# Linear attention and a mixer block on one core: spans of 384 and 288, tensor-engine tiles of 32 and 64 rows or columns, a new instruction order

## The chip, the cores and the metric

The kernel runs on one core of a Trainium2 chip. The metric is device time in microseconds (us). The engines are named as the profile names them: PE is the tensor engine's matrix multiply and PEld its weight load, DVE the vector engine, ACT the scalar engine, POOL the GpSimd engine, SP the engine that issues all DMAs here.

## The reference

Batch 4, 4 heads, sequence 1088, head dimension 32; the mixer works on 128 channels (4 heads of 32), with 256 token units and 1536 channel units.

```python
def phi(x):                                  # 8 x 8 = 64 features of one head
    a = np.einsum('rd,bhsd->bhsr', S1, x)
    b = np.einsum('rd,bhsd->bhsr', S2, x)
    return np.einsum('bhsi,bhsj->bhsij', a, b).reshape(*x.shape[:-1], r * r)
q_p, k_p = (phi(q), phi(k))
kv = np.einsum('bhsf,bhsd->bhfd', k_p, v)
z = np.sum(k_p, axis=2)
num = np.einsum('bhsf,bhfd->bhsd', q_p, kv)
den = np.einsum('bhsf,bhf->bhs', q_p, z)[..., None] + 1e-06
x = num / den                                # then (B, S, H * D)
h = np.maximum(x.T @ w_tok1, 0.0) @ w_tok2   # token mixing, per batch
u = x + h.T
out = u + np.maximum(u @ w_ch1, 0.0) @ w_ch2 # channel mixing
```

The four mixer weights arrive as 64-bit floats and are made into 32-bit floats on the chip.

## The kernel before

Every piece of work is an operation with a short name, a cost per engine and a list of what it depends on (`Plan.add`, L153). The order of all operations is written out by hand in the list `ORDER` (L62): `Plan.run` (L166) goes through it, emits each operation on its engine, and adds fills (`fill`, L269: matmuls of the identity into a spare bank) where its costs expect PE idle for more than 400 ns. Each engine then runs its own queue in that order and waits on semaphores. Names with a suffix (`:pool`, `:dve`) say which engine takes an operation that either could do.

The stages, with the names that the text uses:

- **Weights.** 17 pieces of 64-bit words, `w00` to `w04` (first token weight, tiles of 128 rows), `w10` to `w15` (second), `w20` to `w22` and `w30` to `w32` (the two channel weights). Each is loaded (`d00` and so on, L276; the tile is called `doubles`) and converted (`convert`, L283) in six steps: ACT takes the magnitude of the high word (`abs`, L293) and scales the low word (`low`, L297); DVE clamps (`clamp`, L300), shifts into PSUM (`shift`, L304) and puts the sign on (`merge`, L307); POOL adds the two (`add`, L311 and L313). Later each weight is divided into a high and a low half for fast matmuls (`hi` on ACT, L394; `lo` on DVE or POOL, L397).
- **Keys**, `K0` to `K3`, one per batch (`keys`, L411): projections (`K.p`, L424), products on DVE (`K.v`, L443), and sums over the sequence (`K.s`, L460), 36 matmuls each of 64 output rows by 66 columns: for head h the values of both heads of its pair are multiplied, and `blocks` (L470) keeps the half that belongs to the head.
- **Queries.** Batch 0 on PE (`Q0.p`, L539, 12 matmuls with all 128 rows of the transposed queries; the stationary operand `s_spread` is zero for the rows of other heads), with products `Q0.m` on DVE (L560) or POOL (L557). Batches 1 to 3 project 64 rows (`Q.p`, L505, 4 matmuls of 64 x 272), write them to memory (`Q.w`, L599) and read them back repeated (`Q.r`, L612 and L615), then multiply (`Q.m`, L625).
- **Attention and token mixing**, `A0` to `A3` (`mixing`): `A.x` (L645, 36 matmuls), the division `A.d` on DVE, `A.t` (L695 in batch 0, L701 after), `A.w` (L817, L821), residuals `A0.u` (L726), and the division of u into halves, `uh` on ACT (L792) and `ul` on DVE or POOL (L795).
- **Channel mixing**, `U0` to `U11` (`channel_mix`, L856): the 4352 columns of all batches are cut into 12 spans (`_spans`, L40): 384, 384, 320 for batch 0, then eight of 384 and one of 192. For each span and each of 12 blocks of 128 hidden units: three matmuls (`f`, L871), a ReLU into a high part on ACT (`h`, L875), the low part on DVE (`l`, L878), three matmuls (`s`, L884). A span ends with an addition (`ol`, L909) and its store (`out`, L920).

A matmul of 32-bit floats shows as two MATMUL records in the profile, one of the divided halves as one.

Of the kernel before, what the change touches and what calls it, by code (L numbers as in the profile page):

```python
# [67 lines left out]
A0.x0 w03.add Q0.a21 Q0.b21 w10.low w11.abs w20.abs Q0.m21 A0.x1 w04.shift w10.shift A0.d0 A0.d1 w04.merge w11.clamp w04.add w10.merge w11.shift
w20.clamp w11.merge Q1.p Q1.c0 w11.low w30.low w10.add w11.add w13.low w12.abs Q1.c1 w30.abs w20.low w12.low w13.abs A0.x2 A0.d2 A0.t0 A0.t1 A0.t2
A0.relu A0.hT A0.hTh A0.u0 A0.w0 k1 d21 d31 Q1.w0 v1 Q1.w1 d14 d15 d22 d32 q2 w20.shift w12.clamp w30.clamp w20.merge w13.clamp w12.shift w30.shift  # L70
w12.merge w13.shift w30.merge w20.add w20.hi A0.uh00 K1.p w12.add w20.lo:dve w30.add A0.ul00 w13.merge U0.f U0.f A0.u1 U0.f w13.add A0.w1 w00.hi K1.c0
# [919 lines left out]
```

## Time and profile before

| what | value |
|---|---|
| time, median of 3 runs | 224.02 us (223.56 to 224.95) |
| time of the profiled execution | 224.45 us |
| its span, first to last instruction | 222.6 us |
| granted PE clock over the span | 1.000 |
| PE busy | 216.7 us, 97% |
| DVE busy | 151.1 us, 68% |
| ACT, POOL busy | 115.0 us, 60.7 us |

The profiled execution is one run of the program; its time is 1.85 us longer than the span that the instructions cover. Busy time of an engine is the time during which at least one of its instructions is in flight, so a PE that is busy 97% need not be at its peak.

### The profile page before, as it was taken

To read this page: it belongs to the slowest core of one execution; us is meant where nothing else is said; L and a number is where in the kernel's file an instruction comes from. 1 tells how busy PE (TensorE), PEld (TensorE's weight loads), DVE (VectorE), ACT (ScalarE), POOL (GpSimd) and SP (SyncE) were. 2 spreads that over 40 slices of the span, in tenths; PEclk is the share of its full clock that TensorE was granted. 3 is DMA by queue.
4 is the path that set the end of the run, shared out by engine and by line. 5 is a ranking of instruction groups with operands and counts; after the bars stand their busy time and mean duration, and the time that the engine had idled before them with its cause. 6 is when DMAs were issued, how large, how long until landed. Compare 5 with 4: busy or idle time off the path is not lost.

```text
span 222.6 us, 4807 instructions
## 1 busy us (share of the span) xinstructions
PE 216.7 (97%) x1854; PEld 205.5 (92%) x1854; DVE 151.1 (68%) x310; ACT 115.0 (52%) x269; POOL 60.7 (27%) x62
## 2 busy tenths in 40 slices
PE   7999999999999999999999999999999999999994
PEld 7767868789899999999999999999999999999994
DVE  2599999999779854786644667384556654665652
ACT  3488859865826343444533437253554455445441
POOL 2256585578961615102120505000000000000000
PEclk9999999999999999999999999999999999999999
DMA  6999899697059884249550100035000000020001
GB/s 193 417 406 406 248 361 349 214 259 213 9 116 170 256 167 79 65 111 172 197 168 0 38 0 3 0 141 141 3 0 3 35 3 0 0 71 3 35 0 53
DMA packets 10726, 28.41 MB, mean 128 GB/s; under 512 B 1360, under 2 KB 4688, under 8 KB 10704
## 3 DMA queue, kind: packets, MB, share of 16 engines
q1 hardware_dynamic: 10704, 28.11, 41.5%
q8 instruction: 14, 0.23, 0.4%
q14 instruction: 8, 0.07, 0.1%
HBM read 23.27 MB, written 4.83 MB: 126 GB/s over the span
## 4 chain that ended last, share of the span: by engine, by line
PE 79%; DMA 6%; DVE 6%; ACT 3%; issue 2%; SPq 1%; POOL 1%; POOLq 0%; ACTq 0%
PE ps_o L884 29%; PE ps_h L871 28%; DMA br<-rows 5%; PE ps_a L821 4%; PE ps_a L701 3%; PE ps_o L272 3%; PE ps_a L645 3%; PE ps_a L460 2%; DMA doubles<-wt 2%; DVE hl L878 2%; PE ps_a L539 1%; PE ps_h L539 1%; DVE k_p L443 1%; ACT tail L297 1%; PE ps_o L460 1%
## 5 line engine op out<-in xcount | busy, mean ns | idle before, releaser
L875 ACT ACTIVATE hh<-ps_h 128x384 fp32r<-128x384 f32 (+2 forms) x144 | 68.2, 475 | 84.4 <-PE ps_h L871 63.3
L878 DVE SCALAR_TENSOR_TENSOR hl<-ps_h,hh 128x384 fp32r<-128x384 f32 (+2 forms) x144 | 75.3, 532 | 50.3 <-ACT hh L875 46.0
L871 PE MATMUL ps_h<-uh,halves 128*128 128x384 f32 (+2 forms) x288 | 86.0, 333 | 0.6 <-DVE hl L878 0.5
L884 PE MATMUL ps_o<-hh,halves 128*128 128x384 f32 (+2 forms) x288 | 72.0, 332 | 0.0
L871 PEld LDWEIGHTS ps_h<-uh,halves 128*128 128x128 f32 x288 | 53.1, 188 | 1.8 <-DVE hl L878 1.0
L884 PEld LDWEIGHTS ps_o<-hh,halves 128*128 128x128 f32 x288 | 50.6, 188 | 0.6
L871 PE MATMUL ps_h<-ul,halves 128*128 128x384 f32 (+2 forms) x144 | 47.4, 329 | 0.0
L884 PE MATMUL ps_o<-hl,halves 128*128 128x384 f32 (+2 forms) x144 | 47.4, 329 | 0.0
L871 PEld LDWEIGHTS ps_h<-ul,halves 128*128 128x128 f32 x144 | 27.1, 188 | 0.0
L884 PEld LDWEIGHTS ps_o<-hl,halves 128*128 128x128 f32 x144 | 27.1, 188 | 0.0
L625 POOL TENSOR_TENSOR qp<-qp,br 128x544 f32<-128x544 f32 x9 | 13.2, 1484 | 15.9 <-DMA br<-rows 8.7
L311 POOL TENSOR_TENSOR whole<-c,tail 128x512 int32<-128x512 int32 (+3 forms) x11 | 11.7, 1063 | 9.6 <-DVE c L307 8.1
L669 POOL TENSOR_TENSOR xl<-x,xh 128x384 fp32r<-128x384 f32 x6 | 6.1, 1017 | 28.6 <-ACT xh L665 28.6
L293 ACT ACTIVATE c<-doubles 128x512 f32<-128x512 f32 (+3 forms) x17 | 10.3, 624 | 2.5 <-DMA doubles<-wt 2.5
L443 DVE TENSOR_TENSOR k_p<-ps_a,a_sb 128x1024 f32<-128x1024 f32 (+1 forms) x12 | 11.0, 947 | 0.0
L307 DVE SCALAR_TENSOR_TENSOR c<-doubles,ps_h 128x512 int32<-128x512 int32 (+3 forms) x17 | 10.4, 610 | 0.2
L297 ACT ACTIVATE tail<-doubles 128x512 int32<-128x512 uint32 (+3 forms) x17 | 10.4, 630 | 0.1
L304 DVE TENSOR_SCALAR ps_h<-c 128x512 int32<-128x512 int32 (+3 forms) x17 | 10.3, 615 | 0.1
L645 PEld LDWEIGHTS ps_a<-kvz,qp 128*64 128x64 f32 x288 | 9.0, 137 | 1.3 <-issue 0.5
L701 PE MATMUL ps_a<-halves,xh 128*128 128x256 f32 x54 | 10.0, 279 | 0.0
L300 DVE TENSOR_SCALAR c<-c 128x512 f32<-128x512 f32 (+3 forms) x17 | 8.6, 522 | 2.0 <-ACT c L293 1.9
L313 POOL TENSOR_TENSOR c<-c,tail 128x512 int32<-128x512 int32 x6 | 8.1, 1358 | 6.6 <-DVE c L307 3.2
(82 smaller groups left out, 242.2 us busy)
## 6 DMA issues: line engine op xcount, KB each, us to landing
qp<-rows SPq DMA_DIRECT2D x6, 544.0 KB, 8.6
br<-rows SPq DMA_DIRECT2D x12, 272.0 KB
doubles<-wc SPq DMA_DIRECT2D x6, 512.0 KB, 10.8
v_sb<-v SPq DMA_DIRECT2D x4, 594.0 KB, 4.6
k_sb<-kT SPq DMA_DIRECT2D x4, 576.0 KB
q_sb<-qT SPq DMA_DIRECT2D x4, 544.0 KB, 10.4
doubles<-wt SPq DMA_DIRECT2D x4, 512.0 KB, 7.0
xm<-xb SPq DMA_DIRECT2D x3, 576.0 KB, 9.2
```

Of the source, the lines that this page charges most:

```text
L293: nc.scalar.activation(f32(t["c"]), f32(high), AF.Abs)
L297: nc.scalar.activation(t["tail"], low.bitcast(U32), AF.Copy, scale=2.0 ** -29)
L307: nc.vector.scalar_tensor_tensor(t["c"], high, -(1 << 30), t["ps"], op0=ALU.bitwise_and, op1=ALU.bitwise_or)
L311: engines[e].tensor_tensor(dst(), t["c"], t["tail"], op=ALU.add)
L443: nc.vector.tensor_tensor(t["k_p"][:pn, t0 * H:t1 * H], a.unsqueeze(3).broadcast_to([pn, n, R, R]), t["sb", t0][:pn, :n].unsqueeze(2).broa ...
L625: engines[e].tensor_tensor(qp[:, p, cs], qp[:, p, cs], t["br"][:, p, cs], op=ALU.mult)
L645: nc.tensor.matmul(x_ps[c:c + 64, o:o + 2 * (D + 1)], lhsT=qp[:, p, s0 + c:s0 + c + 64], rhs=kvz_all[b % 2][:, p, :], start=True, stop=True,)
L701: nc.tensor.matmul(t["h_ps"][:, :DTOK], lhsT=t[l][:m, i, :], rhs=part(0, piece, r, j * DTOK, DTOK)[:m], start=(i == 0 and k == 0), stop=(i ...
L871: nc.tensor.matmul(h_ps[:, :cn], lhsT=part(2, at[2][e][0], l, at[2][e][1] * P, P), rhs=r[:, :cn], start=(m == 0), stop=(m == 2))
L875: nc.scalar.activation(t["hh"][:, :cn], t["h"][:, :cn], AF.Relu)
L878: nc.vector.scalar_tensor_tensor(t["hl"][:, :cn], t["h"][:, :cn], 0.0, f32(t["hh"][:, :cn]), op0=ALU.max, op1=ALU.subtract)
L884: nc.tensor.matmul(outs[i][:, :cn], lhsT=part(3, at[3][e][0], l, at[3][e][1] * P, P), rhs=r[:, :cn], start=(e == 0 and m == 0), stop=(e == ...
```

## The change

- The last spans: seven of 384 and two of 288 in place of eight of 384 and one of 192.
- `K.s`: each head is multiplied with its own 33 value columns, not with the 66 of its pair. For batches 1 to 3 the 64 features of a head are cut into two matmuls of 32 output rows (72 matmuls of 32 x 33 in place of 36 of 64 x 66). Batch 0 keeps 36, of 64 x 33.
- `Q.p` of batches 1 to 3: eight matmuls of 64 input rows by 32 output rows in place of four of 128 by 64. `Q0.p`: the two head pairs are projected in one operation, each from its own 64 rows, in place of one pair at a time from all 128.
- The conversion: `shift` is gone; `sign` (the sign bit of the high word into PSUM) depends on the load alone; `clamp` has one operation in place of two; `merge` shifts and joins.
- Fills may be 512 columns wide; 36 matmuls of 32 x 8 stand at the program's start.
- Loads have no fixed order among themselves any more, and `ORDER` is another list. The low halves of w20, w12, w01, w10 and w15 move from DVE to POOL with it.

```diff
-    for n in (384,) * 8 + (192,):
+    for n in (384,) * 7 + (288, 288):
...
-s d00 q0 k0 d01 v0 d02 d03 d04 d10 d11 d20 d30 q1 d12 d13 s.abs s.low s.clamp s.shift s.merge s.add Q0.s0:dve Q0.s1:pool w00.abs w00.low w00.clamp
+s q0 d00 d04 d01 k0 s.low s.abs s.clamp s.sign s.merge s.add Q0.s0:dve Q0.s1:dve Q0.p00 Q0.a00 Q0.p01 w00.sign w00.abs Q0.m00 Q0.b01 w00.clamp w04.abs
...
+PAD = 36
...
-            for _ in range(n):
-                nc.tensor.matmul(spare_ps[:, :P], lhsT=ident, rhs=ident, start=True, stop=True)
+            for w in [4] * (n // 4) + [1] * (n % 4):
+                nc.tensor.matmul(spare_ps[:, :w * P], lhsT=ident, rhs=ident.unsqueeze(1).broadcast_to([P, w, P]), start=True, stop=True)
...
-        op = plan.add(name, {"sp": 475.0}, emit, (), takes, uses, boost, order=after)
+        op = plan.add(name, {"sp": 475.0}, emit, (), takes, uses, boost)
...
+        def sign(e):
+            t["ps"] = bank("ps_h")[:, :n].bitcast(I32)
...
+                nc.vector.tensor_scalar(t["ps"], high, -(1 << 31), None, op0=ALU.bitwise_and)
         def clamp(_):
-            nc.vector.tensor_scalar(f32(t["c"]), f32(t["c"]), LEAST, MOST, op0=ALU.max, op1=ALU.min)
-
-        def shift(_):
-            t["ps"] = bank("ps_h").bitcast(I32)[:, :n]
-            nc.vector.tensor_scalar(t["ps"], t["c"], 3, 0x3FFFFFFF, op0=ALU.logical_shift_left, op1=ALU.bitwise_and)
+            nc.vector.tensor_scalar_min(f32(t["c"]), f32(t["c"]), MOST)
         def merge(_):
-            nc.vector.scalar_tensor_tensor(t["c"], high, -(1 << 30), t["ps"], op0=ALU.bitwise_and, op1=ALU.bitwise_or)
+            nc.vector.scalar_tensor_tensor(t["c"], t["c"], 3, t["ps"], op0=ALU.logical_shift_left, op1=ALU.bitwise_or)
...
-                        nc.tensor.matmul(
-                            t["kv"][j * F:(j + 1) * F, p * 2 * (D + 1):(p + 1) * 2 * (D + 1)],
-                            lhsT=t["k_p"][:n, i * H + h].rearrange("p i j -> p (i j)"),
-                            rhs=t["v"][:n, i, 2 * p:2 * p + 2, :].rearrange("p h d -> p (h d)"),
+                        for c in range(parts):
+                            o, m = j * F + c * F // parts, F // parts
+                            nc.tensor.matmul(
+                                t["kv"][o:o + m, p * (D + 1):(p + 1) * (D + 1)],
+                                lhsT=t["k_p"][:n, i * H + h, c * R // parts:(c + 1) * R // parts].rearrange("p i j -> p (i j)"),
+                                rhs=t["v"][:n, i, h, :], start=(i == 0), stop=(i == NT - 1),
...
-        for j in range(2):
-            c = 2 * j + r
-            nc.tensor.matmul(ps[j * 64:(j + 1) * 64, :QC], lhsT=box["s_rows"], rhs=q[:, c * QC:(c + 1) * QC], start=True, stop=True)
+        for c in range(4):
+            for p in range(2):
+                rows = slice(p * 64, (p + 1) * 64)
+                nc.tensor.matmul(ps[p][c * 32:(c + 1) * 32, :QC], lhsT=box["s_rows"][rows], rhs=q[rows, c * QC:(c + 1) * QC], start=True, stop=True)
...
-                        nc.tensor.matmul(x[:, :cn], lhsT=t["s"][:, kind, 2 * p:2 * p + 2].rearrange("p h i j -> p (h i j)"), rhs=box["q_sb", 0][:, cs], start=True, stop=True)
+                        nc.tensor.matmul(
+                            t[kind, g, p][:, :cn], lhsT=t["s"][rows, kind, 2 * p:2 * p + 2].rearrange("p h i j -> p (h i j)"),
+                            rhs=box["q_sb", 0][rows, cs], start=True, stop=True,
...
+    for i in range(PAD):
+        c = i % 4 * 32
+        nc.tensor.matmul(spare_ps[c:c + 32, :8], lhsT=ident[:, c:c + 32], rhs=ident[:, :8], start=True, stop=True)
```

The new list moves instructions. Three places follow. In them `doubles_90` is piece w30, `doubles_91` w12, `doubles_92` w13 and `doubles_93` w21; L305 is `sign`, L308 `clamp`, L311 `merge`, L447 the key products and L817 `ul` in the kernel after, L304, L300, L307, L443 and L795 their counterparts before.

First, DVE just ahead of and behind the first `ul` of span U0. Before:

```order
L307 SCALAR_TENSOR_TENSOR c<-doubles_91,ps_h 128x384
L304 TENSOR_SCALAR ps_h<-c 128x384
L307 SCALAR_TENSOR_TENSOR c<-doubles_90,ps_h 128x512
L397 TENSOR_TENSOR halves_465<-c,halves_465 128x512
L795 TENSOR_TENSOR ul<-ps_a,uh 128x384
L307 SCALAR_TENSOR_TENSOR c<-doubles_92,ps_h 128x384
L443 TENSOR_TENSOR k_p<-ps_a,a_sb 128x1024
```

And now:

```order
L305 TENSOR_SCALAR ps_h<-doubles_92 128x384
L305 TENSOR_SCALAR ps_h<-doubles_93 128x512
L305 TENSOR_SCALAR ps_h<-doubles_90 128x512
L311 SCALAR_TENSOR_TENSOR c<-c,ps_h 128x384
L447 TENSOR_TENSOR k_p<-ps_a,a_sb 128x1024
L308 TENSOR_SCALAR c<-c 128x512 x2
L311 SCALAR_TENSOR_TENSOR c<-c,ps_h 128x512
L817 TENSOR_TENSOR ul<-ps_a,uh 128x384
L311 SCALAR_TENSOR_TENSOR c<-c,ps_h 128x512
```

The merge of w13, the first product of K1, and the sign and the clamp of w21 moved ahead of `ul`; the low half of w20 (`halves_465`) left DVE.

Second, PE around the same place, from the transposes of the hidden units of batch 0 (L735 before) to the first channel matmuls (L871 before); `whole` is a converted piece of the second token weight. Before:

```order
L735 MATMUL ps_a<-ident,h 128x128 x2
L726 MATMUL ps_a<-ident,x 128x128 x3
L817 MATMUL ps_a<-whole_376,hTl 128x384
L817 MATMUL ps_a<-whole_378,hTl 128x384
L424 MATMUL ps_a<-s_c,k_sb 64x64 x18
L871 MATMUL ps_h<-uh,halves_465 128x384
L871 MATMUL ps_h<-ul,halves_465 128x384
```

And now (L757, L428, L748, L839 and L893 are the counterparts of L735, L424, L726, L817 and L871):

```order
L757 MATMUL ps_a<-ident,h 128x128 x2
L428 MATMUL ps_a<-s_c,k_sb 64x64 x18
L748 MATMUL ps_a<-ident,x 128x128 x3
L839 MATMUL ps_a<-whole_506,hTl 128x384
L839 MATMUL ps_a<-whole_432,hTl 128x384
L748 MATMUL ps_a<-ident,x 128x128 x3
L839 MATMUL ps_a<-whole_519,hTl 128x384
L839 MATMUL ps_a<-whole_528,hTl 128x384
L893 MATMUL ps_h<-uh,halves_552 128x384
L893 MATMUL ps_h<-ul,halves_552 128x384
```

The second transposes and the second token product of batch 0, which stood behind the first channel matmuls, now stand ahead of them.

Third, PE at the projection of Q2 and the sums of K1. Before:

```order
L871 MATMUL ps_h<-uh,halves_465 128x384
L505 MATMUL ps_a<-q_sb,s_rows 64x272 x4
L460 MATMUL ps_a<-v_sb,k_p 64x66 x36
L424 MATMUL ps_a<-s_c,k_sb 64x64 x18
L871 MATMUL ps_h<-uh,halves_465 128x384
```

And now:

```order
L893 MATMUL ps_h<-uh,halves_552 128x384
L512 MATMUL ps_a<-q_sb,s_rows 32x272 x8
L467 MATMUL ps_a<-v_sb,k_p 32x33 x72
L893 MATMUL ps_h<-uh,halves_552 128x384
```

The projection and the sums have twice the matmuls, of smaller tiles, and the projection of K2 (L424) has left this place for a later one of its own.

## Rows read from the trace of the kernel before

**Rows 1.** The page: busy time, share and instructions of each engine.

```profile
PE 216.7 (97%) x1854; PEld 205.5 (92%) x1854; DVE 151.1 (68%) x310; ACT 115.0 (52%) x269; POOL 60.7 (27%) x62
```

**Rows 2.** Busy time of each engine in stretches of 10 us.

```profile
core 0: us, PE busy (x) PEld busy (x) DVE busy (x) ACT busy (x) POOL busy (x), PEclk, DMA share, GB/s
...
30.00:40.00 10.00, 10.00 (x101) 8.17 (x101) 9.97 (x19) 8.73 (x22) 6.20 (x6) 1.00 0.98 345
40.00:50.00 10.00, 9.36 (x131) 8.45 (x127) 9.72 (x18) 7.29 (x20) 7.26 (x6) 1.00 0.82 245
50.00:60.00 10.00, 10.00 (x115) 9.26 (x113) 8.86 (x14) 7.59 (x19) 8.98 (x8) 1.00 0.44 124
```

**Rows 3.** The chain of waits from 31 to 48 us, by line.

```profile
by line: DMA doubles<-wt 23.1%; DVE hl L878 20.1%; issue 17.8%; DVE k_p L443 15.3%; DVE c L300 11.9%; DVE c L307 10.9%; DVE ps_h L304 9.0%; DVE ul L795 6.4%; PE ps_h L871 4.7%; PE ps_o L884 1.0%
```

**Rows 4.** Timeline from 0 to 11 us: start, length, instruction, idle time before it.

```profile
1.36 6.70 PE L272 MATMUL ps_o<-ident 128*128 128x128 f32 x32 [1.36 <-POOL ident masks.py:199]
...
5.54 0.67 ACT L293 ACTIVATE c<-doubles 128x512 f32<-128x512 f32 x1 [2.54 <-DMA doubles<-wt]
...
7.90 0.81 PE L539 MATMUL ps_a<-q_sb,s_spread 128*128 128x384 f32 x2
...
9.46 0.56 DVE L560 TENSOR_TENSOR qp<-xT,ps_h 128x384 f32<-128x384 f32 x1 [1.34 <-PE ps_h L539]
...
10.54 0.49 DVE L560 TENSOR_TENSOR qp<-xT,ps_h 128x320 f32<-128x320 f32 x1 [0.52 <-PE ps_h L539]
```

**Rows 5.** Timeline from 30 to 38 us, DVE.

```profile
30.89 0.73 DVE L397 TENSOR_TENSOR halves<-c,halves 128x512 fp32r<-128x512 f32 x1
31.54 0.55 DVE L795 TENSOR_TENSOR ul<-ps_a,uh 128x384 fp32r<-128x384 f32 x1
32.01 0.54 DVE L307 SCALAR_TENSOR_TENSOR c<-doubles,ps_h 128x384 int32<-128x384 int32 x1
...
34.87 0.42 DVE L300 TENSOR_SCALAR c<-c 128x512 f32<-128x512 f32 x1
...
35.67 0.68 DVE L304 TENSOR_SCALAR ps_h<-c 128x512 int32<-128x512 int32 x1
...
37.32 1.22 DVE L443 TENSOR_TENSOR k_p<-ps_a,a_sb 128x1024 f32<-128x1024 f32 x1
```

**Rows 6.** Timeline from 31.5 to 35 us, PE.

```profile
31.97 0.44 PE L871 MATMUL ps_h<-uh,halves 128*128 128x384 f32 x1
...
33.12 0.49 PE L726 MATMUL ps_a<-ident,x 128*128 128x128 f32 x3
...
33.98 1.45 PE L817 MATMUL ps_a<-whole,hTl 128*128 128x384 f32 x4
```

**Rows 7.** The chain of waits in order of time, whole program: start, length, what.

```profile
8.06 0.65 PE ps_a L539 x2
...
15.70 2.27 PE ps_o L460 x72
...
56.74 2.25 PE ps_a L460 x72
58.99 0.72 PE ps_o L884 x3
...
80.38 0.88 PE ps_h L871 x6
81.26 1.07 PE ps_a L505 x8
...
204.21 1.56 PE ps_o L884 x9
...
218.19 1.35 PE ps_o L884 x12
```

**Rows 8.** Timeline from 11.60 to 11.70 us, PE.

```profile
11.65 0.28 PE L424 MATMUL ps_a<-s_c,k_sb 128*64 128x64 f32 x2
```

**Rows 9.** Line L424 by itself: count, shortest, median and longest in ns, first and last start.

```profile
L424 PE MATMUL ps_a<-s_c,k_sb x144: 220/222/270, 11.7 to 66.3; 128*64 128x64 f32 x144
```

**Rows 10.** Timeline from 54 to 56 us, POOL.

```profile
54.42 1.30 POOL L397 TENSOR_TENSOR halves<-whole,halves 128x512 fp32r<-128x512 f32 x1
```

More of the change, by code (lines that the diff above doesn't have):

```diff
@@ L68 @@
[L68 to L71, printed above, removed]
@@ new lines @@
+w04.clamp w00.merge Q0.p20 Q0.p21 Q0.a01 Q0.a20 Q0.p10 Q0.m01 Q0.m20 s.rows w01.abs Q0.a21 Q0.a10 K0.p d02 w04.low Q0.b21 w04.sign w01.clamp w01.sign
+w04.merge w01.merge w02.sign v0 d03 d11 d20 d10 d12 d13 k1 q1 d21 d30 Q0.p11 Q0.m21 w00.low w00.add w04.add K0.c0 w02.low K0.c4 K0.c8 w01.low w01.add
+K0.v0 Q0.m10 K0.v4 K0.v8 w02.abs w03.abs w02.clamp w03.clamp w02.merge w03.low Q0.a11 w11.abs Q0.b11 w11.clamp w03.sign w11.sign Q0.m11 w03.merge
+w02.add w11.merge K0.s00 K0.s04 K0.s08 K0.s10 K0.s14 K0.s18 K0.kvz A0.x0 w10.abs A0.d0 A0.x1 A0.d1 A0.x2 A0.t0 A0.t1 w03.add A0.d2 w10.sign w11.low
@@ new lines @@
+Q1.p w11.add w12.abs w13.abs w10.low w20.abs w20.low Q1.c0 Q1.c1 A0.t2 A0.relu A0.hT w10.clamp w13.clamp w12.clamp w20.sign w20.clamp w12.sign
+w10.merge d31 d14 Q1.w0 q2 v1 Q1.w1 w20.merge w12.merge K1.p d15 d32 d22 Q1.r0None Q1.r00 Q1.r01 Q1.r1None Q1.r10 Q1.r11 w10.add w20.add w13.low
+w12.low w30.abs A0.hTh K1.c0 w12.add w13.sign w21.sign w30.sign w13.merge w13.add K1.v0 A0.u0 A0.w0 A0.u1 A0.w1 w21.low K1.c4 w30.low w21.abs w20.hi
+A0.uh00 w30.clamp w21.clamp w20.lo:pool w30.merge A0.ul00 w21.merge w31.abs w31.low w13.hi K1.c8 K1.v4 K1.v8 U0.f U0.f U0.f w30.add A0.uh11 U0.h U0.h
@@ new lines @@
+w30.hi w21.add Q2.p A0.ul11 w31.clamp U0.l U0.l w31.sign w31.merge w30.lo:pool K1.s U1.f U0.h w14.low w21.hi w21.lo:pool w14.abs w15.abs U1.h U0.l
+w31.add U1.l w14.sign w22.low w22.abs Q2.c0 w14.clamp w15.clamp w14.merge U0.s U1.f U0.s U0.s U1.f U1.s U0.f U1.h w31.hi U1.h w15.low U0.h Q2.c1
+w00.hi U1.l w22.clamp w15.sign U1.l U0.l w15.merge w31.lo:pool w14.add w22.sign w22.merge U1.s A0.u2 U1.s U0.s U0.f U0.f w15.add A0.w2 U0.h w01.hi
+U0.h w32.abs w32.low U0.l w22.add w32.sign U0.l w32.clamp w32.merge w22.hi Q1.m00:pool w22.lo:pool w32.add Q1.m10:pool Q1.m01:pool U0.s U1.f U1.f U0.s
@@ L316, in convert @@
         r = plan.add(name + ".low", act_sb(n), rest, [loaded], [tail_hold])
+        g = plan.add(name + ".sign", dve(n), sign, [loaded], [ps_hold])
         m = plan.add(name + ".clamp", dve2(n), clamp, [a], (), [c_hold], port=True)
[L318 to L319 removed]
+        m = plan.add(name + ".merge", dve(n), merge, [m, g], (), [c_hold, ps_hold])
         ways = {"dve": 69 + 2.084 * n} if keep else {"pool": 141 + 2.15 * n}
@@ L583, in project @@
                 t["ps", r] = bank("ps_a")
-                project_queries(box["q_sb", b], r, t["ps", r])
-        p = plan.add(f"{n}.p", {"pe": 2 * 2 * QC / 1.2}, project, [q_loaded[b], s_rows_done], ps, [q_hold[b]], boost, 1, order=[after])
+            project_queries(box["q_sb", b], [t["ps", r] for r in range(2)])
+        p = plan.add(f"{n}.p", {"pe": 2 * (QC / 1.2 + 40)}, project, [q_loaded[b], s_rows_done], ps, [q_hold[b]], boost, 2, order=[after])
         for r in range(2):
```

141 lines of the change are left out of this document (73 added, 68 removed).

## The prediction

> **What bounds the kernel now.** I read the page first: PE is busy 97% of the span [rows 1], so at first sight the time is the sum of PE's work. The table of stretches splits this. From 30 to 50 us DVE is busy 9.97 and 9.72 of 10 us, and PE shows 9.36 in the second of these [rows 2]. The chain of waits for 31 to 48 us runs almost wholly over DVE lines and the loads, with 4.7% and 1.0% on PE [rows 3]: PE's queue is full there, but with instructions that DVE releases. From 50 us on PE is busy 10.00 [rows 2], and the end of the chain is PE alone [rows 7]. So I cut the time at the first channel matmul of span U0, at 31.97 us [rows 6]. What comes before is set by DVE, which has to convert weights; what comes after is mainly PE's own work; its last matmul ends at 218.19 + 1.35 = 219.54 us [rows 7]. That leaves 222.6 - 219.54 = 3.06 us for the last addition and store. So before = 31.97 + 187.57 + 3.06.
>
> **The middle: PE's work behind the first channel matmul.**
>
> *Spans.* Three matmuls per block, two layers, 12 blocks make 72 matmuls for a span. One of 384 columns takes 1.56 / 9 = 0.1733 us, one of 320 takes 0.88 / 6 = 0.1467, one of 192 takes 1.35 / 12 = 0.1125 [rows 7]. A 384 and a 192 cost 72 x 0.2858 = 20.6 us. For 288 the line through 384 and 320 gives 0.1334, the line through 320 and 192 0.1382, so two spans of 288 cost 19.2 to 19.9 us. The gain is 0.7 to 1.4; I take 1.3, since 288 is nearer to 320.
>
> *Sums of K1 to K3.* They cost 2.25 us each, 72 records, 36 rounds with two tiles abreast, 0.0625 us a round [rows 7]. The query projection, also two abreast, takes 1.07 / 4 = 0.2675 us a round with 272 columns [rows 7]. Time goes with columns: (0.2675 - 0.0625) / (272 - 66) = 1.0 ns a column and nothing fixed. With 33 columns a round takes about 0.031 us; 144 records at four abreast are 36 rounds, 1.1 us. No row shows four tiles abreast. The other end is that a record costs 2.25 / 72 = 0.031 us however small it is: 144 x 0.031 = 4.5 us. Between the ends, two records of different tiles start close together: two took 0.28 us in all [rows 8], where one lasts up to 0.270 [rows 9], so some 10 ns apart; four in 40 ns would give 1.4 us. I take 1.2, near to the column rule: 3 x 1.05 = 3.15 us gained; the ends are a gain of 3.4 and a loss of 6.8.
>
> [...]
>
> *Projections Q2 and Q3.* Eight tiles abreast make two rounds of 0.2675, 0.53 us in place of 1.07. Tiles that share columns and differ in rows occur nowhere in this trace, so the ends are 0.5 gained each and, if row tiles took turns, nothing. I take 2 x 0.53 = 1.06 gained.
>
> *Work that moves ahead of the cut.* One transposed residual, at most 0.49, less what overlaps, about 0.3, and one token product: four records of 384 columns at 0.65 a pair, 1.3 us [rows 6, 7]. 1.6 us leave the middle.
>
> *Changes of tile shape.* Behind the sums three second-layer matmuls take 0.72 where 3 x 0.1733 = 0.52 are due [rows 7], so a change costs about 0.2 us. By the order the middle had 14 such changes and now has 18: K2's projection stands alone, and projection and sums, adjacent twice, differ in shape. That costs 0.8.
>
> *Waits on DVE.* PE sits visibly idle for 0.64 us from 40 to 50 us [rows 2]. The order now converts w13 and most of w21 ahead of the cut, so I let this go.
>
> Middle: 187.57 - 1.3 - 3.15 - 1.06 - 1.6 + 0.8 - 0.64 = 180.6 us.
>
> **The front: when the first channel matmul can run.** PE's savings here (Q0.p halved, 12 matmuls of about 0.65 us, 0.54 for the short ones; K0.s halved from 2.27 us [rows 7]) need not show, because DVE decides. DVE runs two long conversions of the front behind each other and its first `ul` ends at 32.09 us [rows 5]. To its list ahead of that `ul` the order adds the sign of w21 (0.68, as a `shift` of that size), its clamp (0.42), the merge of w13 (0.54) and K1's first product (1.22); it takes off the low half of w20 (0.73) [rows 5]: +2.1 us. `sign` costs what `shift` cost, same size and destination; the clamp is as long with one operation as with two, as far as I can bound it (0 to 0.42 less). Off the list go waits: DVE sat idle 1.34 and 0.52 us for the first query products [rows 4]. Those came late because 32 records of fills held PE until 7.90 us [rows 4]. At 6.70 / 16 = 0.42 us a fill, the seven fills' worth that remain ahead of Q0, with 36 small matmuls of some 0.5 to 1.3 us, let it start near 5.5 us if the queries have landed, and they are now loaded first. But the first weight, which had landed by 5.54 [rows 4], comes behind them. I take half of the 1.86 us, 0.9. The cut moves to 31.97 + 2.1 - 0.9 = 33.2 us; ends 31.3 (all idle gone and overlap of instructions counted) and 35.
>
> Free loads and the shorter chain from load to merge I cost at nothing: DVE's full queue covers them. If that cover were gone, each would pull the front forward, and the second rival prices that. `clamp` and `merge` now wait for ACT and for `sign`; what is queued behind them on DVE is more conversions, and ahead of the cut only PE waits for those, with fills.
>
> **The tail.** The last addition has 288 columns, not 192, and the store half as many bytes again: +0.1, 3.16 us.
>
> **The sum.** 33.2 + 180.6 + 3.16 = 217.0 us of span. The profiled execution took 224.45 for a span of 222.6, and the median of the runs lies 0.43 under the profiled one; so 217.0 + 1.85 - 0.43 = 218.4 us. The likeliest case has its own range of 216 to 221.
>
> **The rivals.**
>
> *PE sets the front too.* From 7.90 to 31.97 PE spent 24.1 us. Without 3.6 of Q0.p, 1.1 of K0.s and 0.5 of Q1.p, with the 1.6 that moved in and nine more changes of shape (1.8), it needs 22.3 us from 5.5 on: the cut at 28 to 30, 4 us earlier, and 214.5 us in all. For it: PE is also busy in the front. Against it: DVE's 9.97 of 10 [rows 2], and DVE's list grew. Chance 0.22.
>
> *Small tiles are paced by their number.* At 0.031 us a record the sums take 4.5 us, 3.3 more than I count, three times: 218.4 + 9.9 = 228.3, slower. It decides from a sum of 1.2 + 5.6 / 3 = 3.1 us on, where the whole gain is gone. For it: 31 ns a record is what the trace shows on average. Against it: the proportion to columns, and two records 10 ns apart [rows 8, 9]. [...] Chance 0.10.
>
> *POOL becomes late.* Five low halves (512, 384, 512, 384 and 320 columns) move to POOL, where 512 take 1.30 us [rows 10]: 2112 / 512 x 1.30 = 5.4 us. POOL was busy 8.98 of 10 us from 50 to 60 [rows 2], and `A1.t` and `A1.w` wait for these halves; behind them in POOL's queue stand the query products of the next batch, for which `A2.x` waits. If two thirds of it show, 218.4 + 3.6 = 222.0, no change that can be told. Against it: POOL was lightly used after 60 us, and PE has channel work to put in between. Chance 0.13.
>
> **How the numbers follow.** The forecast keeps 0.55. About 1% either way is what a measurement can tell here, so faster means below 221.8 and slower above 226.3. Faster: 0.55 and 0.22, nearly all of both: 0.76. The small-tile case gives slower 0.09; the rest, 0.15, is within 1%. The range from 213.5 to 222.5 takes in the case in which PE sets the front, the late ends of the front, and POOL's case; it leaves out the small tiles' and the far ends of the others.
>
> **What would show each step.** The groups by line: `K.s` of K1 to K3 at 1.1 to 1.4 us (over 3 us and the small tiles decide); projections Q2 and Q3 near 0.53; 288-column matmuls near 0.134. The timeline: the first channel matmul near 33 us with DVE full ahead of it; at 29 the first rival holds. The waits: PE on `lo` and `xl` of POOL in 55 to 75 us would speak for the third. I am wrong if the sums are slower than 2.25 us, if PE's granted clock falls in the front, or if PE stands idle for more than 2 us behind 50 us.

## The result, and the profile after

The kernel after takes 222.09 us (median of 5 runs, 221.66 to 222.46), beside 224.28 us for the kernel before on the same chip: a ratio of 0.990 (0.987 to 0.993). Forecast were 218.4 us; the range of 213.5 to 222.5 holds the time, but the gain is 2.2 us where 5.6 were forecast. Here and below a time is the median of all runs of a kernel, while a ratio leaves out runs more than 1.5% above its fastest one, which moves the ratio of some kernels with stops. The profiled execution took 222.09 us for a span of 220.3. Its three parts:

| part | before | forecast | after |
|---|---|---|---|
| front, to the first channel matmul of U0 | 31.97 | 33.2 | 32.89 |
| middle, to the end of the last matmul | 187.57 | 180.6 | 184.1 |
| tail | 3.06 | 3.16 | 3.3 |

The page's first line answers to [rows 1]:

```profile
PE 212.3 (96%) x2162; PEld 197.5 (90%) x2162; DVE 148.5 (67%) x305; ACT 114.8 (52%) x270; POOL 62.9 (29%) x67
```

The busy times in stretches of 10 us, as [rows 2]:

```profile
30.00:40.00 10.00, 8.72 (x186) 5.67 (x184) 9.79 (x17) 8.36 (x20) 8.24 (x8) 1.00 0.98 316
40.00:50.00 10.00, 9.80 (x52) 8.70 (x52) 8.43 (x18) 7.69 (x18) 6.75 (x7) 1.00 0.64 202
50.00:60.00 10.00, 9.28 (x111) 8.64 (x110) 7.67 (x17) 6.81 (x18) 8.87 (x7) 1.00 0.39 144
```

PE works 4.4 us less than before, but in 30 to 60 us it is now idle for 2.2 us, where it had been idle for 0.64. The chain of waits over 31 to 48 us, by line, answers to [rows 3]:

```profile
by line: DMA doubles<-wc 68.3%; issue 11.2%; DVE ps_h L305 10.1%; DVE c L311 6.5%; ACT c L294 3.3%; DVE hl L900 2.7%; DVE c L308 2.5%; ACT hh L897 2.3%; ACT abT L613 2.2%; ACT tail L298 0.2%; ACTq L897 0.1%
```

Before, DVE lines filled it; now a load of the channel weights (`doubles<-wc`) does. The whole chain in order of time gives that load and the durations that answer to [rows 7]: `Q.p` is L512, `K.s` L467, the 288-column matmuls the last row.

```profile
25.05 0.62 PE ps_a L512 x16
...
29.77 11.61 DMA doubles<-wc
...
80.65 0.62 PE ps_a L512 x16
81.27 1.36 PE ps_a L467 x137
...
215.39 1.61 PE ps_o L906 x12
```

The timeline of PE, DVE and ACT from 32 to 52 us shows where PE stands still (start, length, instruction, idle time before it and what ended it):

```profile
32.89 0.64 PE L893 MATMUL ps_h<-uh,halves 128*128 128x384 f32 x1
...
34.85 0.64 PE L512 MATMUL ps_a<-q_sb,s_rows 64*32 64x272 f32 x2
...
35.63 0.21 PEld L512 LDWEIGHTS ps_a<-q_sb,s_rows 64*32 64x32 f32 x14 [0.65 <-ACT halves L398]
...
35.90 1.45 DVE L308 TENSOR_SCALAR c<-c 128x512 f32<-128x512 f32 x1
...
36.27 1.45 PEld L467 LDWEIGHTS ps_a<-v_sb,k_p 128*32 128x32 f32 x144 [0.44 <-DVE ul L817]
36.28 1.56 PE L467 MATMUL ps_a<-v_sb,k_p 128*32 128x33 f32 x144
...
38.33 0.44 PE L893 MATMUL ps_h<-uh,halves 128*128 128x384 f32 x1 [0.49 <-DVE hl L900]
...
40.12 0.44 PE L893 MATMUL ps_h<-uh,halves 128*128 128x384 f32 x1 [0.48 <-DVE hl L900]
...
41.41 0.67 ACT L298 ACTIVATE tail<-doubles 128x512 int32<-128x512 uint32 x1 [1.76 <-DMA doubles<-wc]
...
43.33 0.56 DVE L900 SCALAR_TENSOR_TENSOR hl<-ps_h,hh 128x384 fp32r<-128x384 f32 x1 [1.54 <-ACT hh L897]
...
48.73 1.53 DVE L308 TENSOR_SCALAR c<-c 128x512 f32<-128x512 f32 x1
...
51.04 0.44 PE L893 MATMUL ps_h<-uh,halves 128*128 128x384 f32 x1 [0.72 <-DVE c L311]
```

Three things hold PE up. Q2's projection starts, and then its weight loads (PEld) wait 0.65 us for ACT; those of K1's sums wait 0.44 us for DVE, but PE is still at work on the projection then. Next come DVE's clamps (L308): the ones at 35.90 and 48.73 last 1.45 and 1.53 us where the median is 0.42. They delay what stands behind them in DVE's queue: first the `hl` of the waits at 38.33 and 40.12, then the merge (L311) that ends the wait at 51.04. That merge gives back a bank of `ps_h`, and the matmul that waits writes to one; in the new conversion `sign` takes the bank ahead of the clamp. And ACT stands for 1.76 us at a step of the conversion of w22 or w32, whose load lands only at 41.4; the ReLU parts `hh` stand behind it in ACT's queue, DVE's `hl` behind those, PE's second layer behind these.

The middle can be split by PE's records: each is given the time from the end of the one before to its own end, and in channel and mixer work what exceeds the median of its kind by more than 0.06 us goes to a row of its own (us):

| class | before | forecast, change | after | change |
|---|---|---|---|---|
| channel matmuls (spans) | 144.39 | -1.3 | 142.47 | -1.92 |
| sums K1 to K3 | 6.45 | -3.15 | 4.21 | -2.24 |
| projections Q2, Q3, waits inside included | 2.13 | -1.06 | 2.05 | -0.08 |
| moved ahead of the cut | 3.68 | -1.6 | 2.06 | -1.62 |
| waits and changes of shape | 3.42 | +0.16 | 5.42 | +2.00 |
| the rest (`K.p`, `A.x`, `A.t`, `A.w`) | 27.50 | 0 | 27.89 | +0.39 |

The sum is -3.5 where -7.0 were forecast. Of the difference of 3.5 us, 1.8 are waits, 1.0 the projections, 0.9 the sums, 0.4 the rest; the spans gave 0.6 more than forecast.

### The profile page after: what moved, and what is told of

It is laid out like the page before. It is cut to its first block, busy times and chain, and to the rows that moved or that the text cites. A ratio compares the mean times of both kernels' runs of the same rounds, so it can differ in the third digit from the quotient of the medians.

```text
span 220.3 us, 5412 instructions
## 1 busy us (share of the span) xinstructions
PE 212.3 (96%) x2162; PEld 197.5 (90%) x2162; DVE 148.5 (67%) x305; ACT 114.8 (52%) x270; POOL 62.9 (29%) x67
## 4 chain that ended last, share of the span: by engine, by line
PE 80%; DVE 8%; DMA 5%; issue 2%; ACT 2%; SPq 1%; POOL 0%; POOLq 0%; ACTq 0%; DVEq 0%
PE ps_o L906 31%; PE ps_h L893 30%; DMA doubles<-wc 5%; PE ps_a L723 4%; PE ps_a L843 4%; PE ps_a L667 3%; PE ps_a L717 2%; DVE ps_h L305 2%; DVE c L308 2%; PE ps_o L273 2%; DVE c L311 1%; PE ps_a L467 1%; DVE k_p L447 1%; PE ps_a L428 1%; PE ps_a L552 1%
## 5 line engine op out<-in xcount | busy, mean ns | idle before, releaser
L893 PE MATMUL ps_h<-uh,halves 128*128 128x384 f32 (+2 forms) x288 | 86.0, 331 | 1.7 <-DVE hl L900 1.0
L893 PEld LDWEIGHTS ps_h<-uh,halves 128*128 128x128 f32 x288 | 53.0, 188 | 2.7 <-DVE hl L900 1.4
L893 PE MATMUL ps_h<-ul,halves 128*128 128x384 f32 (+2 forms) x144 | 47.1, 327 | 0.0
L817 POOL TENSOR_TENSOR ul<-us,uh 128x384 fp32r<-128x384 f32 (+5 forms) x10 | 6.6, 664 | 93.3 <-ACT uh L814 86.1
L893 PEld LDWEIGHTS ps_h<-ul,halves 128*128 128x128 f32 x144 | 27.1, 188 | 0.2 <-DVE ul L817 0.2
L305 DVE TENSOR_SCALAR ps_h<-doubles 128x512 int32<-128x512 int32 (+3 forms) x17 | 10.3, 622 | 2.1 <-DMA doubles<-wt 2.1
L447 DVE TENSOR_TENSOR k_p<-ps_a,a_sb 128x1024 f32<-128x1024 f32 (+1 forms) x12 | 11.2, 949 | 0.2 <-ACT a_sb L438 0.2
L647 POOL TENSOR_TENSOR qp<-qp,br 128x544 f32<-128x544 f32 x8 | 10.8, 1367 | 0.0
L311 DVE SCALAR_TENSOR_TENSOR c<-c,ps_h 128x512 int32<-128x512 int32 (+3 forms) x17 | 10.1, 611 | 0.1
L401 POOL TENSOR_TENSOR halves<-c,halves 128x512 fp32r<-128x512 f32 x6 | 8.7, 1461 | 4.6 <-ACT halves L398 4.1
L273 PE MATMUL ps_o<-ident 128*128 128x128 f32 (+1 forms) x36 | 8.6, 369 | 1.4 <-POOL ident masks.py:199 1.4
```

The costliest lines, as they stand in the source:

```text
L273: nc.tensor.matmul(spare_ps[:, :w * P], lhsT=ident, rhs=ident.unsqueeze(1).broadcast_to([P, w, P]), start=True, stop=True)
L305: nc.vector.tensor_scalar(t["ps"], high, -(1 << 31), None, op0=ALU.bitwise_and)
L311: nc.vector.scalar_tensor_tensor(t["c"], t["c"], 3, t["ps"], op0=ALU.logical_shift_left, op1=ALU.bitwise_or)
L447: nc.vector.tensor_tensor(t["k_p"][:pn, t0 * H:t1 * H], a.unsqueeze(3).broadcast_to([pn, n, R, R]), t["sb", t0][:pn, :n].unsqueeze(2).broa ...
L647: engines[e].tensor_tensor(qp[:, p, cs], qp[:, p, cs], t["br"][:, p, cs], op=ALU.mult)
L893: nc.tensor.matmul(h_ps[:, :cn], lhsT=part(2, at[2][e][0], l, at[2][e][1] * P, P), rhs=r[:, :cn], start=(m == 0), stop=(m == 2))
```

## The experiments

Diffs are against the kernel after where nothing else is said. Ratios are to the kernel before, with 95% intervals; the kernel after stands at 0.990 (0.987 to 0.993).

**The tensor work, one part undone at a time.** First the sums of K1 to K3 as 36 matmuls of 64 rows by 33 columns:

```diff
-                    parts = 2 if b else 1
+                    parts = 1
```

> The changed kernel with the sums of K1 to K3 in tiles of 64 output rows by 33 columns (36 matmuls each, not 72 of 32 x 33). If a matmul's time goes with its columns, as the prediction had it, these sums stay near 1.2 to 1.5 us and the time stays at 222.1. If a tile of 64 rows has a pace of its own, as the sums of K0 show now (72 records, 2.5 us with 33 columns), they go back to about 2.1 us: +0.65 us for each sum that PE paces. All three count: 224.0; only K2 and K3, because 33 to 52 us is paced by others: 223.4.

Measured 223.93 us, ratio 0.999 (0.998 to 1.001), as if all three sums counted: the split into 32-row tiles is worth 0.9%, 2.1 us, nearly the whole gain of the change. In the trace the sums are 2.46 us longer and the middle 1.9; what K1's part is worth is tested by itself further below. The line of the sums by itself, in this kernel and then in the kernel after (least, median, longest in ns, first and last start):

```profile
L467 PE MATMUL ps_a<-v_sb,k_p x216: 223/223/245, 36.1 to 127.8; 128*64 128x33 f32 x108
```

```profile
L467 PE MATMUL ps_a<-v_sb,k_p x432: 191/197/218, 36.3 to 126.1; 128*32 128x33 f32 x144
```

Three sums took 6.67 us with 64-row tiles of 33 columns, and 6.45 with 66 columns before: half the columns saved nothing. What saved time is the 32-row tile: with four abreast, 144 records take 1.43 to 1.56 us, 10 to 11 ns a record. Whether that comes of four tiles abreast in place of two, or of the shorter weight loads (109 ns in place of 138), no run separates.

Then the old last spans:

```diff
-    for n in (384,) * 7 + (288, 288):
+    for n in (384,) * 8 + (192,):
```

> The changed kernel with the spans of before (eight of 384, one of 192). PE alone paces the end, so the whole difference of the matmuls' times must show: 72 x (0.1733 + 0.1125) against 144 x 0.1333 us is +1.4 us, by the sums of both traces +1.9: 223.5 to 224.0. A rival in which the chain of ScalarE and VectorE sets the last spans gives 222.1, no change.

Measured 222.9 us, ratio 0.995 (0.993 to 0.997): 0.5% over the kernel after, 1.1 us, less than the 1.4 to 1.9 expected. In the trace the channel matmuls take 143.93 us, 1.46 more than in the kernel after. So the two spans of 288 give what the line through 384 and 320 said; the other 0.5 us of the 1.92 in the table is about a nanosecond a matmul between two traces, and not the spans.

And the old projections of Q1 to Q3:

```diff
-        for c in range(4):
-            for p in range(2):
-                rows = slice(p * 64, (p + 1) * 64)
-                nc.tensor.matmul(ps[p][c * 32:(c + 1) * 32, :QC], lhsT=box["s_rows"][rows], rhs=q[rows, c * QC:(c + 1) * QC], start=True, stop=True)
+        for j in range(2):
+            c = 2 * j + r
+            nc.tensor.matmul(ps[j * 64:(j + 1) * 64, :QC], lhsT=box["s_rows"], rhs=q[:, c * QC:(c + 1) * QC], start=True, stop=True)
```

> The changed kernel with the projections Q1 to Q3 of before (four matmuls of 128 rows by 64, 1.07 us, where eight of 64 by 32 take 0.62). If only what lies behind 52 us counts, Q3 alone shows: +0.45 us, 222.5. If PE paces everywhere, three times: +1.35, 223.4. If the new tiles cost more in changes of shape than they save, it becomes faster: 221.6.

Measured 222.54 us, ratio 0.992 (0.989 to 0.995), not to be told from the kernel after. Q3's projection does fall, from 1.07 to 0.62 us; Q2's saving goes into the waits around it.

**The order alone.** The kernel before, with the new sums, spans and projections of Q1 to Q3 and nothing else (the diff, against the kernel before, in part):

```diff
-    for n in (384,) * 8 + (192,):
+    for n in (384,) * 7 + (288, 288):
...
+        parts = 2 if b else 1
```

> The kernel before with its order, conversion, loads, fills and Q0 untouched, and with the new spans, sums and projections Q1 to Q3. If the new order and conversion cost time of their own (first channel matmul 0.9 us later, waits of PE on VectorE 3.2 us in place of 1.6), this kernel is faster than the changed one: 224.3 - 1.9 (spans) - 2.2 (sums) - 0.5 (projections) = 219.7. If the small tiles have a cost that the order of the change hides, or PE's savings vanish in waits here too: 221 to 222. If the order brings the gain and the tiles nothing: 224.

Measured 222.4 us, ratio 0.990 (0.988 to 0.993), nearer to the case of savings that vanish in waits than to 219.7. Four of the six runs took 221.42 to 222.41, the profiled one 226.04 and one 229.97. The profiled one shows a thing that no theory had. PE's timeline at K3's sums:

```profile
81.06 1.06 PE L463 MATMUL ps_a<-v_sb,k_p 128*32 128x33 f32 x101
84.93 0.58 PE L463 MATMUL ps_a<-v_sb,k_p 128*32 128x33 f32 x43 [2.81 <-issue]
```

and the stretches of 2 us behind it, columns as in [rows 2]:

```profile
84.00:86.00 2.00, 1.07 (x47) 1.02 (x48) 0.29 (x1) 0.00 (x0) 0.25 (x1) 0.99 0.52 112
86.00:88.00 2.00, 2.00 (x11) 1.96 (x9) 0.44 (x1) 0.17 (x1) 2.00 (x2) 0.50 0.39 104
```

PE stops in the middle of the sums for 2.81 us, waiting for nothing that the profile shows; then the granted clock is 0.50. The stop could be the fetch of instructions: the page of the kernel after counts 17 transfers of 16 KB on an instruction queue, for 4324 records of PE and PEld, one for about 254 records; with the 32 instructions of PE's sequencer in that trace it is one for 256:

```profile
q8 instruction: 17, 0.28, 0.5%
```

So the next runs moved the block ends.

**The block ends.** The kernel after without its 36 small matmuls at the start:

```diff
-PAD = 36
+PAD = 0
```

> The changed kernel without the 36 small matmuls at the start (the fills behind them become three wide ones' worth more). In the kernel with the old order and the new tiles PE stopped for 2.81 us in the middle of a sum of small tiles, with nothing to wait for but its own instructions, while a 16 KB block of the instruction queue was on its way, and its granted clock then fell to 0.50 for some 3.4 us. If the place of the block ends decides, this kernel, whose blocks end 140 instructions elsewhere, shows such a stop in one of its sums: 2 to 5 us longer, 224 to 227, in the trace as idle time before L467 put down to issue. If the stop there had another cause, or the 36 matmuls do nothing: 222.1, give or take 0.5.

Measured 226.05 us (223.41 to 229.51), ratio 1.005 (1.001 to 1.009): a little slower than before, and far more scattered. K1's sums on PE's timeline:

```profile
34.92 1.39 PE L467 MATMUL ps_a<-v_sb,k_p 128*32 128x33 f32 x123
38.66 0.39 PE L467 MATMUL ps_a<-v_sb,k_p 128*32 128x33 f32 x21 [2.35 <-issue]
```

A second stop, of 1.9 us, follows K2's sums (`A.w`, L843). This fits two readings: the place of the block ends, or that the small matmuls keep PE busy at the start. A 32-bit matmul is four records here, two on PE and two on PEld, so 64 of them are one block; the next kernel has 67 at the start and three fills fewer, 64 more matmuls ahead of K1's sums than the one with none:

```diff
-PAD = 36
+PAD = 67
```

> 67 small matmuls at the start in place of 36. With three fills fewer that puts 64 32-bit matmuls more ahead of K1's sums than the kernel with none of them had: 256 records, one 16 KB instruction block exactly, so the block ends fall on the same instructions as there. If it is the place of the block ends that counts, the stop comes back: K1's sums stand still for 2 to 3 us near their 120th record, the granted clock falls behind it, and the time is that of the kernel without the small matmuls (226.05) within 1.5 us, 3 to 5 us over the kernel after. If the small matmuls help because they keep PE busy at the start, more of them help as much: no stop, and the time is that of the kernel after (222.1) within 1 us.

Measured 226.93 us (225.37 to 229.8), ratio 1.011 (1.006 to 1.016). The stop is back, at the same record (and so is the second one, 2.0 us behind K2's sums):

```profile
36.50 1.37 PE L467 MATMUL ps_a<-v_sb,k_p 128*32 128x33 f32 x123
39.96 0.51 PE L467 MATMUL ps_a<-v_sb,k_p 128*32 128x33 f32 x21 [2.10 <-issue]
...
40.88 0.52 PE L893 MATMUL ps_h<-ul,halves 128*128 128x384 f32 x1
41.20 0.52 PE L893 MATMUL ps_h<-uh,halves 128*128 128x384 f32 x1
41.52 0.84 PE L906 MATMUL ps_o<-hh,halves 128*128 128x384 f32 x2
```

Behind it matmuls of 384 columns start 0.32 us apart, where 0.17 is usual, and the stretches of 2 us show the clock:

```profile
40.00:42.00 2.00, 2.00 (x26) 1.93 (x27) 0.27 (x1) 0.24 (x1) 1.16 (x1) 0.52 0.63 173
42.00:44.00 2.00, 2.00 (x10) 2.00 (x9) 1.72 (x5) 1.99 (x5) 0.00 (x0) 0.63 0.50 181
```

So the place of the block ends decided here, and not the work at the start. The old order with 36 small matmuls moved the stop as well:

```diff
+    for i in range(PAD):
+        c = i % 4 * 32
+        nc.tensor.matmul(spare_ps[c:c + 32, :8], lhsT=ident[:, c:c + 32], rhs=ident[:, :8], start=True, stop=True)
```

> The kernel before with its old order and the new spans, sums and projections Q1 to Q3 (as before), and in addition 36 small matmuls at the start, in place of three fills. If block ends decide on the stop of 2.81 us in K3's sums, they lie elsewhere now and the stop and the fall of the clock behind it are gone, in all runs: 221.5, none above 223. If the stop comes wherever small tiles run fast, it stays: some runs at 226 to 230.

Measured 223.27 us (222.45 to 227.93), ratio 0.997 (0.993 to 1.001). The expectation failed in part: nothing stops at K3, but nine of the twelve runs lie above 223, and `K.p` of K2, right behind K1's sums, stands for 1.07 us on "issue":

```profile
43.74 0.74 PE L425 MATMUL ps_a<-s_c,k_sb 128*64 128x64 f32 x17 [1.07 <-issue]
```

Its block ends were then put a quarter of a block away from the run with none (18 small matmuls in place of 36):

```diff
-PAD = 36
+PAD = 18
```

> The order, conversion, loads and Q0 of before with the new sums, spans and projections of Q1 to Q3, and 18 small matmuls at the start, which move the block ends by a quarter of a block against the run without them: the sums of K1, K2 and K3 then begin 43, 31 and 33 records into a block, near the 79 and 29 that ran without a stop in the kernel after. If stops hid what the old order can do (2.8 us and 1.5 us of lower clock in the profile of the run without small matmuls), no stop shows and the time is 218.5 to 220: the new order then costs 2 us or more. If old and new order are worth the same, no stop shows and the time is 221.4 to 222.4. If a stop shows at another place, nothing is told.

Measured 222.35 us (221.37 to 223.26), ratio 0.994 (0.991 to 0.997), without a stop. Without a stop the old order lies 0.35% (0.8 us) behind the new, with intervals that overlap: new order, conversion and loads are worth that or nothing, and the rest of the gain is the tensor work's. The longest wait of PE near 44 us is 1.28 us here, where it was 0.62 before the tensor work got shorter.

**What K1's saving is worth.** K1's sums alone in 64-row tiles:

```diff
-                    parts = 2 if b else 1
+                    parts = 2 if b > 1 else 1
```

> The kernel after, with K1's sums alone in 64-row tiles of 33 columns (36 matmuls, 2.2 us in place of 1.56). If the waits on ACT and DVE at 38 to 46 us swallow what the small tiles save there, nothing or at most 0.2 us is lost: 222.1 to 222.3, and the wait at 38.8 us falls by about the 0.65 us that the sums grow. If the saving counts in full, 222.7 to 222.9.

Measured 225.83 us, ratio 1.008 (1.005 to 1.011): neither. Fewer records in K1 move the block ends behind it, and the waits of PE name the place, just behind K2's sums:

```profile
PE ps_a L843 <- issue: 2.1, 1, 2.1
```

So the same with 9 small matmuls at the start, which puts K2's and K3's sums back to the places in their blocks that they have in the kernel after:

```diff
-PAD = 36
+PAD = 9
...
-                    parts = 2 if b else 1
+                    parts = 2 if b > 1 else 1
```

> The kernel after with K1's sums in 64-row tiles, and 9 small matmuls in place of 36, so that K2's and K3's sums begin at the same places in their blocks as in the kernel after. No stop. If the waits from 38 to 52 us swallow K1's saving of 0.65 to 0.75 us, the time is that of the kernel after within 0.3 us (221.8 to 222.4) and those waits are some 0.6 us shorter; if it counts in full, 222.7 to 222.9.

Measured 221.58 us (221.37 to 221.77), ratio 0.990 (0.988 to 0.991): K1's sums grow from 1.56 to 2.3 us and the time doesn't. The time alone does not prove it, for the front of this profile is 31.78 us, and kernels with the same front as the kernel after have it anywhere from 31.91 to 33.23. The timeline does:

```profile
35.20 2.29 PE L467 MATMUL ps_a<-v_sb,k_p 128*64 128x33 f32 x72
37.42 0.45 PE L893 MATMUL ps_h<-uh,halves 128*128 128x384 f32 x1
...
39.01 0.44 PE L893 MATMUL ps_h<-uh,halves 128*128 128x384 f32 x1 [0.28 <-DVE hl L900]
```

From the start of K1's sums to the end of the second wait behind them it is 3.81 us here and 3.84 in the kernel after (36.28 to 40.12): the first of the two waits is gone, the second shorter, and the whole 0.74 us is swallowed by then. PE's waits from 37 to 53 us are 2.76 us, 3.20 in the kernel after.

**The loads and the clamps.** The loads of w32 and w22, which K1's projection preceded, moved ahead of w14's:

```diff
-w10.merge d31 d14 Q1.w0 q2 v1 Q1.w1
+w10.merge d31 d32 d22 d14 Q1.w0 q2 v1 Q1.w1
...
-K1.p d15 d32 d22 Q1.r0None
+K1.p d15 Q1.r0None
```

> The changed kernel with the loads of w32 and w22 ahead of those of q2, v1 and w14 and of the writes of Q1. In the changed kernel ScalarE waits 1.76 us at 41.4 us for one of them, with two ReLUs behind it in its queue, and PE then loses 0.70 us. If that order of the loads is what costs there: the wait is gone and the time is 0.4 to 0.8 shorter, 221.3 to 221.7. If VectorE would hold PE anyway: 222.1. If the later q2 and v1 hold up K1's sums and Q2: longer, 222.5 to 223.

Measured 220.3 us, ratio 0.984 (0.979 to 0.988), and again beside the last runs:

> The same kernel as f3_loads_early again, beside the other three on one chip: 220.0 to 220.8 if the gain of 1.8 us holds.

220.97 us, ratio 0.987 (0.984 to 0.989). ACT's wait has gone to another load:

```profile
ACT c L294 <- DMA doubles<-wt: 1.8, 1, 1.8
```

but it ends earlier, and the three waits of PE between 43 and 46 us are gone: 37 to 53 us have 1.97 us of waits. The gain is larger than the 0.4 to 0.8 us expected. The traces put 0.8 and 0.9 us of it in the middle, where the waits are; the front is 31.88 us in one profile and 32.89, as in the kernel after, in the other, so the rest is scatter there. All nine runs (219.8 to 221.41) are faster than all runs of both kernels.

All 18 clamps left out, so that words above the largest value would not be held there:

```diff
-            nc.vector.tensor_scalar_min(f32(t["c"]), f32(t["c"]), MOST)
+            pass
```

> The changed kernel with the clamp left out of all conversions (it changes no value that lies in the range, so for these inputs nothing). VectorE loses 17 operations of 0.30 to 0.42 us, of which some took 1.5 us. If VectorE paces the stretch up to 52 us, the first channel matmul comes 2 us earlier or more, and PE's waits between 33 and 52 us (3.2 us) halve: 218.0 to 219.5. If loads, ScalarE or POOL pace it, the time stays within 0.5 of 222.1.

Measured 220.78 us, ratio 0.985 (0.981 to 0.989), between the two cases expected: the waits at 38 to 41 us are nearly gone (0.2 us) and the front is 0.7 us shorter, within its scatter, but the wait behind the late load grows to 1.5 us, and PE's waits from 37 to 53 us fall to 2.42 only. Both together, again without the clamps:

> Both: the loads of w22 and w32 early (1.8 us) and the 18 clamps left out (1.3 us). Two limits beside each other, so that each hides part of the other: more than the sum, 218.5 or less. One and the same limit, gone with either: 220 to 220.5. Independent: 219.

Measured 218.95 us, ratio 0.978 (0.974 to 0.982). By the times the gains add up or do a little more (1.3 and 1.1 to 1.8 alone, 3.1 together), which does not tell independent limits from limits that hide each other. The waits do: PE's from 37 to 53 us fall from 3.20 us by 0.8 without the clamps, by 1.2 with the early loads, and by 2.8, to 0.37 us, with both. Each limit hides part of the other, as the grown wait behind the late load already showed.

To keep the clamp and lose its stretch, the three long ones were given the form of `merge`:

```diff
-            nc.vector.tensor_scalar_min(f32(t["c"]), f32(t["c"]), MOST)
+            if name in ("w11", "w31", "w32"):
+                nc.vector.scalar_tensor_tensor(f32(t["c"]), f32(t["c"]), MOST, f32(t["c"]), op0=ALU.min, op1=ALU.min)
+            else:
+                nc.vector.tensor_scalar_min(f32(t["c"]), f32(t["c"]), MOST)
```

> The kernel after, with the clamps of w11, w31 and w32 (the three that lasted 1.03 to 1.53 us beside POOL's work) as a three-operand instruction with the minimum taken twice, like the form of merge, which never stretched. If that form does not give way to POOL: each lasts 0.55 to 0.7 us, 2 us less in all on DVE, of which 0.5 to 1 us shows in the time (leaving all 18 clamps out gave 1.3 us): 221.1 to 221.6. If the stretch comes with POOL's work whatever the form, they stay at 1 to 1.5 us and the time is that of the kernel after.

Measured 222.09 us, ratio 0.992 (0.988 to 0.995), as the kernel after. The three by themselves:

```profile
L309 DVE SCALAR_TENSOR_TENSOR c<-c x3: 550/1734/1792, 17.4 to 48.5; 128x512 f32<-128x512 f32 x2, 128x384 f32<-128x384 f32 x1
```

The two beside POOL's work stretch all the more, to 1.73 and 1.79 us, so it is not the form of the clamp. In the kernel after, the clamp at 35.90 us starts 0.14 us behind a `lo` on POOL:

```profile
35.76 2.72 POOL L401 TENSOR_TENSOR halves<-c,halves 128x512 fp32r<-128x512 f32 x2
```

Those are two instructions, of 1.30 and 1.46 us; the first ends at 37.06, and the clamp at 37.35, 0.29 us behind it. So the clamp lasts as if it had waited for the POOL instruction ahead of it. In the traces of the two kernels eleven clamps begin while an instruction of POOL runs, and each ends 0.15 to 0.31 us behind that instruction's end; the long ones, of 1.08, 1.45 and 1.53 us after and 1.06, 1.31 and 0.86 before, began early in theirs. That they wait for POOL is inferred from these times.

The same form for two clamps together with the early loads:

> The two loads early, as before (1.8 us faster than the kernel after), and the two clamps that still stretched there (w31, w32) in the three-operand form. If loads and clamps hold PE up at different places, the gains add: 219.3 to 219.9 us. If the waits only pass from one to the other, 220.3 as with the early loads alone.

Measured 221.74 us, ratio 0.989 (0.985 to 0.992), outside both cases expected: no gain over the early loads, rather a loss.

## Why the prediction was wrong, step by step

*Cut and front: right in mechanism, in the number partly by luck.* 33.2 us forecast, 32.89 measured, with DVE busy 9.93 of the 10 us ahead of it. Up to the end of the first `ul` (32.09 us before, 33.18 after) DVE's busy time grew by 1.5 us where 2.1 were forecast, and its idle time fell by 0.4 where 0.9 were; the two errors cancel:

```profile
0.00:32.09 32.09, 29.99 (x316) 23.89 (x316) 24.78 (x55) 21.46 (x49) 15.73 (x23) 1.00 0.91 335
```

```profile
0.00:33.18 33.18, 30.54 (x399) 21.96 (x399) 26.30 (x59) 22.55 (x53) 16.11 (x23) 1.00 0.89 336
```

How exact such a cut can be shows in the kernel with early loads: its two profiles have it at 31.88 and 32.89 us.

*Spans, work that moved, tail: right*, with 1.92 for 1.3 (1.46 by the experiment with the old spans), 1.62 for 1.6, and 3.3 for 3.16 us.

*Sums: right in direction, mis-sized, for a wrong reason.* The step "time goes with columns ... and nothing fixed" fails: K0's sums, 64 rows by 33 columns, still go at 31 ns a record, and so did those of K1 to K3 in the first experiment. What helped is the 32-row tile, not fewer columns. Four abreast took 10 to 11 ns a record, as two records 10 ns apart [rows 8, 9] had said; 144 records are 1.43 to 1.56 us, not 1.2. That pace, 1.4 us, stood in the text between the two ends and was not taken. The rival that paced small tiles by their number, at 31 ns a record, is out.

*Projections: half wrong.* What was counted as two rounds of eight tiles abreast took 0.62 us in place of 1.07, near the 0.53. But Q2's stands where PE waits for ACT and DVE, and saves nothing there.

*Waits: the step that failed.* "The order now converts w13 and most of w21 ahead of the cut, so I let this go." With that the sum took PE's 0.64 us of waiting off. The waits grew from 1.6 to 3.2 us between 37 and 53 us. There were two faults in it. PE was counted as the bound of the whole middle, though [rows 2, 3] showed DVE full until 50 us: what PE saves before that point turns into waits, as K1's sums show (0.74 us longer, and level again within 3.8 us) and the old order's wait of 1.28 us. And free loads, which the text "cost at nothing", had DVE's queue named as their cover; the late load is not on DVE's way but on ACT's, where the ReLU parts stand behind the conversion. (The text says that the second rival prices the loss of that cover; it is the first, and only for a front that comes earlier.) Of the 1.6 us by which the waits grew, K1's saving is 0.7 and the late load, by the three waits that go with it, another 0.7. The long clamps are not new: the kernel before has three as well, of 1.06, 1.31 and 0.86 us, where the kernel after has 1.08, 1.45 and 1.53. They are a limit in both.

*The rival "PE sets the front too"* is out with the cut at 32.89. *"POOL becomes late"* gave the right time, 222.0, for a wrong reason: no PE wait of 50 us or later ends with POOL. POOL does matter, by the clamps of 1.45 and 1.53 us that ran beside it, where the median is 0.42.

*What no step had:* the instruction blocks. The 36 small matmuls were costed at "some 0.5 to 1.3 us" of the front; they take 1.08 us there by the chain, and without them the kernel is slower than before, through two stops of 2.35 and 1.9 us. That the new order as it stands has no stop is luck as far as the prediction goes: nothing in it depends on where the blocks end.

## What to carry to other kernels

Cut a program where its bound changes before you add up what an edit saves: only savings behind that point count in full. Where a queue carries both conversions and work that the next engine waits for, look at which load its next instruction needs, also on the engine that has time to spare. And here PE stopped for 1.1 to 2.8 us inside or right behind long runs of very short matmuls, at places that moved with the number of instructions ahead: with 36 small matmuls at the start the time was 222.09 us, with none it was 226.05, with 67 it was 226.93. An experiment that changes the number of matmuls must be read with that in mind.
